# Closing a kernel without a block: engines run straight from the main program, closing waits in issue order, the last store waited for at the very end

## Chip, cores, metric

One core of one Trainium2 chip. The metric is the device time of one execution in microseconds (us). The profile's span, from the first instruction recorded to the last, is a little shorter than that time (the difference: "time minus span"). Every run quoted here is fast, with a mean granted TensorE clock of 0.997 or more.

## The reference, cut to what matters

Tokens x (2048 x 640) go through linear attention with 32 heads of 20 and through a gated feed-forward network of width 1728; a gate mixes the two.

```python
g = sigmoid((x * gate_w).sum(-1, keepdims=True))
a = A_ref(x, A_wqkv, A_w_phi, A_wo)     # q, k, v; softmax features; kv state; num / den; wo
b = (gelu(x @ w_gate) * (x @ w_up)) @ w_down
return g * a + (1 - g) * b
```

## The kernel before

The kernel records each operation through a small helper, which adds the waits: a semaphore counts each engine's finished operations, and each DMA takes one of 16 "lanes" of SyncE in turn, each lane with its own semaphore. `finish` makes one engine wait for everything. In the code, `_Ev` is a semaphore together with the value that it has to reach. All of it was written inside the SyncE part of a block (`nc.Block`).

```python
    def _wait(self, eng, ev):                      # skips what this engine has already waited for
        w = self.seen.setdefault(id(eng), {})
        if ev.value <= w.get(id(ev.sem), 0):
            return
        w[id(ev.sem)] = ev.value
        eng.wait_ge(ev.sem, ev.value)
    ...
    def finish(self, eng):                         # lanes 0..15 first, then the engines
        for q in self.queues.values():
            for L in q["lanes"]:
                if L["count"] > 0:
                    eng.wait_ge(L["sem"], L["count"])
        for e in self.engs.values():
            if e["count"] > 0:
                eng.wait_ge(e["sem"], e["count"])
    ...
    def run(self):
        nc = self.nc
        self.alloc()
        with nc.Block() as blk:
            @blk.sync
            def _(sp):
                self.sc = _Sched(nc, {"sp": (nc.sync, 16), "act": (nc.scalar, 4), "pool": (nc.gpsimd, 2)})
                self.loads()
                self.attention_state()
                self.ffn()
                self.sc.finish(sp)
```

The very last output tile is stored in two pieces; the second, 128 columns wide (32 KB), is the last store of the program, and it happens to use lane 7.

The softmax here doesn't subtract the row's maximum and nothing guards it: scores larger than these inputs give would overflow.

Of the kernel before, what the change touches and what calls it, by code (L numbers as in the profile page):

```python
# [11 lines left out]
class _Ev:  # L12
    __slots__ = ("sem", "value", "ekey")

    def __init__(self, sem, value, ekey=None):
        self.sem = sem
        self.value = value
        self.ekey = ekey


class _Sched:


    def __init__(self, nc, dma_lanes):
        self.nc = nc
        self.engs = {}
        for key, obj in (("pe", nc.tensor), ("act", nc.scalar), ("dve", nc.vector), ("pool", nc.gpsimd)):
            self.engs[key] = {"obj": obj, "sem": nc.alloc_semaphore(f"ev_{key}"), "count": 0}
        self.queues = {}
        for q, (eng, nl) in dma_lanes.items():  # L30
            lanes = [{"sem": nc.alloc_semaphore(f"dq_{q}_{i}"), "count": 0} for i in range(nl)]
            self.queues[q] = {"lanes": lanes, "rr": 0, "eng": eng}
        self.seen = {}
        self.bufs = {}

    def _wait(self, eng, ev):
        w = self.seen.setdefault(id(eng), {})
# [4 lines that stand above are left out]
# [39 lines left out]
    def dma(self, qkey, fn, reads=(), writes=(), guard=()):  # L81
        q = self.queues[qkey]
        lane = q["rr"]
        q["rr"] = (lane + 1) % len(q["lanes"])
        L = q["lanes"][lane]
        if L["count"] > 0:
            self._wait(q["eng"], _Ev(L["sem"], L["count"]))
        for ev in self._hazards(reads, list(writes) + list(guard)):
            self._wait(q["eng"], ev)
        fn(q["eng"]).then_inc(L["sem"], 16)  # L90
        L["count"] += 16
        self._record(reads, writes, (qkey, lane), _Ev(L["sem"], L["count"]))

    def finish(self, eng):
        for q in self.queues.values():
            for L in q["lanes"]:
                if L["count"] > 0:
                    eng.wait_ge(L["sem"], L["count"])
        for e in self.engs.values():
            if e["count"] > 0:  # L100
                eng.wait_ge(e["sem"], e["count"])


class _Kernel:
# [22 lines left out]
    def run(self):  # L127
        nc = self.nc
        self.alloc()
        with nc.Block() as blk:  # L130
            @blk.sync
            def _(sp):
                self.sc = _Sched(nc, {"sp": (nc.sync, 16), "act": (nc.scalar, 4), "pool": (nc.gpsimd, 2)})
                self.loads()
                self.attention_state()
                self.ffn()
                self.sc.finish(sp)

    def alloc(self):
        nc = self.nc  # L140
# [669 lines left out]
```

## Time and profile before

| | before |
|---|---|
| time, median of the 3 runs known at first | 299.86 us (299.65 to 300.2) |
| span of the profiled run | 297.8 us |
| TensorE busy | 98% of the span |
| TensorE's last matmul starts | 294.85 us |
| last store issued / its semaphore complete | 295.55 / 296.99 us |
| last instruction ends | 297.82 us |

From the page of the kernel before: span, TensorE's row, and the chain of waits that ended last.

```profile
span 297.8 us, 4821 instructions
PE 292.9 (98%) x1913; PEld 171.9 (58%) x1913; DVE 162.2 (54%) x318; ACT 104.3 (35%) x183; POOL 29.0 (10%) x58
PE 96%; DMA 1%; ACT 1%; issue 0%; SPq 0%; ACTq 0%
```

TensorE bounds everything between the first and the last matmul. So a change that touches no compute has to look for its gain at the two ends.

What SyncE waited for in the last 14 us, kernel before (waiting line, what released it, us in total, times, longest; two waits for the last results before the store are left out):

```profile
...
SPq L98 <- DMA out_dram<-outsb: 0.9, 1, 0.9
SPq L130 <- PEq L130: 0.2, 1, 0.2
```

L98 is the lane loop of `finish`, L101 its engine loop, L130 the block. Their instructions in the kernel before (engine, operation, count, nanoseconds min/median/max, first and last start in us), line by line:

```profile
L98 SPq EVENT_SEMAPHORE  x7: 17/28/842, 295.9 to 297.1; - x7
L101 SPq EVENT_SEMAPHORE  x4: 28/28/28, 297.2 to 297.3; - x4
L130 POOLq EVENT_SEMAPHORE  x2: 17/17/17, 297.6 to 297.7; - x2
...
L130 SPq COMPARE_BRANCH  x1: 41/41/41, 297.4 to 297.4; - x1
L130 SPq DRAIN  x1: 13/13/13, 297.6 to 297.6; - x1
L130 SPq EVENT_SEMAPHORE  x1: 17/17/17, 297.8 to 297.8; - x1
...
L130 PEldq EVENT_SEMAPHORE  x1: 51/51/51, 297.8 to 297.8; - x1
```

One of the seven L98 waits lasts 842 ns: that is the wait that really waits, for the last store. The other ten find their semaphores long reached, and yet they take time. The records of the trace, in order, make it plain (the compiler packs up to two waits into an instruction):

```
start us   ns   kernel before, SyncE unless noted
295.546   333   issue of the last store
295.924    17   wait            } four waits that pass at once
...                             }
296.170   842   wait, holds lane 7 (last store); lane 7 completes at 296.990
297.044    28   wait            } six waits that pass at once,
...                             } 61 ns from start to start
297.348    28   wait            }
297.413    41   branch out of the block (holds one more wait)
297.590    13   drain, start of the closing barrier of five engines
297.765    51   last release of the barrier, on TensorE; ends 297.816
```

From the landing of the last store to the end of the span: 0.83 us in which no data is computed or moved.

### The profile page before, as it was taken

To read this page: it belongs to the slowest core of one execution; us is meant where nothing else is said; L and a number is where in the kernel's file an instruction comes from. 1 tells how busy PE (TensorE), PEld (TensorE's weight loads), DVE (VectorE), ACT (ScalarE), POOL (GpSimd) and SP (SyncE) were. 2 spreads that over 40 slices of the span, in tenths; PEclk is the share of its full clock that TensorE was granted. 3 is DMA by queue.
4 is the path that set the end of the run, shared out by engine and by line. 5 is a ranking of instruction groups with operands and counts; after the bars stand their busy time and mean duration, and the time that the engine had idled before them with its cause. 6 is when DMAs were issued, how large, how long until landed. Compare 5 with 4: busy or idle time off the path is not lost.

```text
span 297.8 us, 4821 instructions
## 1 busy us (share of the span) xinstructions
PE 292.9 (98%) x1913; PEld 171.9 (58%) x1913; DVE 162.2 (54%) x318; ACT 104.3 (35%) x183; POOL 29.0 (10%) x58
## 2 busy tenths in 40 slices
PE   7999999999999999999999999999999999999996
PEld 3576656555544556775555577655457765545763
DVE  1348999998875679514655700455580045567000
ACT  3367787576663221121222212122221212232111
POOL 7000000000000011201011100101110010111000
PEclk9999999999999999999999999999999999999999
DMA  7999990000002122112011200201101010110101
GB/s 219 211 209 335 355 350 18 0 0 2 0 2 53 35 20 28 47 44 66 3 22 22 20 27 24 60 6 25 22 9 37 22 46 23 22 24 0 44 24 44
DMA packets 38098, 18.77 MB, mean 63 GB/s; under 512 B 30203, under 2 KB 37820, under 8 KB 38076
## 3 DMA queue, kind: packets, MB, share of 16 engines
q1 hardware_dynamic: 37424, 18.44, 24.4%
q8 instruction: 15, 0.25, 0.3%
q10 hardware_dynamic: 652, 0.03, 0.1%
q14 instruction: 7, 0.06, 0.1%
HBM read 8.96 MB, written 2.62 MB: 39 GB/s over the span
## 4 chain that ended last, share of the span: by engine, by line
PE 96%; DMA 1%; ACT 1%; issue 0%; SPq 0%; ACTq 0%
PE ps L616 37%; PE ps L694 20%; PE ps L359 13%; PE ps L700 7%; PE ps L504 7%; PE ps L649 4%; PE ps L452 3%; PE ps L368 2%; PE ps L626 1%; DMA xtok<-in_A_x_dram 1%; PE ps L339 1%; ACT Eq L510 1%; ACT Ek L418 0%; PE ps L284 0%; PE ps L304 0%
## 5 line engine op out<-in xcount | busy, mean ns | idle before, releaser
L616 PE MATMUL ps<-xT,wu_sb 128*128 128x512 bf16 x260 | 64.6, 379 | 0.2 <-ACT Eq L510 0.2
L616 PE MATMUL ps<-xT,wg_sb 128*128 128x512 bf16 x260 | 64.6, 379 | 0.0
L694 PE MATMUL ps<-wd_sb,hT 128*128 128x320 bf16 (+2 forms) x448 | 63.6, 299 | 0.0
L621 DVE TENSOR_TENSOR hT<-ps,gl 128x512 bf16<-128x512 f32 x52 | 35.7, 688 | 44.5 <-PE ps L616 44.4
L619 ACT ACTIVATE gl<-ps 128x512 bf16<-128x512 f32 x52 | 31.1, 597 | 80.8 <-PE ps L616 78.6
L694 PEld LDWEIGHTS ps<-wd_sb,hT 128*128 128x128 bf16 x448 | 43.2, 98 | 17.8
L616 PEld LDWEIGHTS ps<-xT,wu_sb 128*128 128x128 bf16 x260 | 25.4, 98 | 31.1 <-issue 0.7
L359 PE MATMUL ps<-w,xT 128*128 128x512 bf16 (+3 forms) x240 | 40.9, 321 | 0.0
L616 PEld LDWEIGHTS ps<-xT,wg_sb 128*128 128x128 bf16 x260 | 25.0, 98 | 27.2
L710 ACT ACTIVATE outsb<-ps,Gm 128x640 bf16<-128x640 f32 (+2 forms) x17 | 13.0, 763 | 74.7 <-PE ps L700 74.7
L678 POOL TENSOR_TENSOR Og<-O,O 128x640 bf16<-128x640 bf16 x16 | 22.3, 1394 | 167.5 <-DVE O L676 167.5
L359 PEld LDWEIGHTS ps<-w,xT 128*128 128x128 bf16 x240 | 22.4, 97 | 18.2
L665 DVE RECIPROCAL RH<-ps 128x32 f32<-128x32 f32 x16 | 5.7, 358 | 40.7 <-PE ps L649 39.7
L429 DVE TENSOR_REDUCE Dk<-Ek 128x64 f32<-128x1280 bf16 x16 | 23.7, 1480 | 3.2 <-ACT gcol L421 3.2
L438 DVE TENSOR_TENSOR Ek<-Ek,Dk 128x640 bf16<-128x640 bf16 x32 | 25.0, 821 | 0.6
L504 PE MATMUL ps<-xT,wq 128*128 128x512 bf16 x100 | 24.7, 379 | 0.3 <-ACT Eq L510 0.3
L676 DVE TENSOR_TENSOR O<-ps,RH 128x640 bf16<-128x640 f32 x32 | 24.8, 816 | 0.0
L700 PE MATMUL ps<-wo_sb,goT 128*128 128x320 bf16 (+2 forms) x160 | 24.5, 299 | 0.0
L510 ACT ACTIVATE Eq<-ps 128x512 bf16<-128x512 f32 x40 | 21.7, 604 | 4.0 <-PE ps L504 4.0
L418 ACT ACTIVATE Ek<-ps 128x640 bf16<-128x640 f32 x32 | 20.7, 702 | 3.5 <-PE ps L359 3.5
L700 PEld LDWEIGHTS ps<-wo_sb,goT 128*128 128x128 bf16 x160 | 15.5, 98 | 6.3
L649 PEld LDWEIGHTS ps<-KV,Eq 128*128 128x128 bf16 x192 | 12.0, 98 | 3.1
(66 smaller groups left out, 154.2 us busy)
## 6 DMA issues: line engine op xcount, KB each, us to landing
out_dram<-outsb SPq DMA_DIRECT2D x15, 160.0 KB, 2.0
wd_sb<-in_B_w_down_dram SPq DMA_DIRECT2D x1, 2080.0 KB, 12.4
wg_sb<-in_B_w_gate_dram SPq DMA_DIRECT2D x1, 1120.0 KB, 5.7
wu_sb<-in_B_w_up_dram SPq DMA_DIRECT2D x1, 1120.0 KB, 9.6
wg_sb<-in_B_w_gate_dram SPq DMA_DIRECT2D x1, 960.0 KB, 9.9
wu_sb<-in_B_w_up_dram SPq DMA_DIRECT2D x1, 960.0 KB, 10.2
w<-in_A_wqkv_dram SPq DMA_DIRECT2D x5, 160.0 KB, 4.0
wo_sb<-in_A_wo_dram SPq DMA_DIRECT2D x1, 800.0 KB, 10.1
```

Source lines behind the costliest of these rows:

```text
L359: sc.op("pe", lambda e, kt=kt: e.matmul(self.bank(bank)[:, bcol:bcol + n], self.xT[:, kt, t * P:(t + 1) * P], self.w3[:, kt, c0:c0 + n], s ...
L429: sc.op("dve", lambda e: e.tensor_reduce(self.Dk[:, se, 0, :].rearrange("p (s h) -> p s h", h=H), self.Ek[:, se, :, :].rearrange("p s (h d ...
L438: sc.op("dve", lambda e, v=v, r=r: e.tensor_tensor(v, v, r, ALU.mult), reads=[("Rk", se)], writes=[("Ek", se, s)])
L504: sc.op("pe", lambda e, kt=kt: e.matmul(self.bank(bank), self.wq2[:, kt, i * P:(i + 1) * P], self.xT[:, kt, b * self.BT:(b + 1) * self.BT] ...
L510: sc.op("act", lambda e, s=s, scale=scale: e.activation(self.Eq[:, s, i, b * self.BT:(b + 1) * self.BT], self.bank(bank), AF.Exp, scale=sc ...
L616: sc.op("pe", lambda e, kt=kt, w=w, bk=bk: e.matmul(self.bank(bk), w[:, kt, c * P:(c + 1) * P], xs(kt), start=(kt == 0), stop=(kt == self. ...
L619: sc.op("act", lambda e: e.activation(self.gl[:, slot, :], self.bank(banks[0]), AF.Gelu_apprx_tanh), reads=[("ps", banks[0])], writes=[("g ...
L621: sc.op("dve", lambda e: e.tensor_tensor(self.hT[:, c, :], self.bank(banks[1]), self.gl[:, slot, :], ALU.mult), reads=[("ps", banks[1]), ( ...
L649: sc.op("pe", lambda e, s=s, i=i, n=n, o0=o0, k0=k0, bk=bk, r=r: e.matmul(self.bank(bk)[:, o0:o0 + n], self.Eq[:, s, i, t * P:(t + 1) * P] ...
L676: dve(lambda e, o=o, f=f, s=s: e.tensor_tensor(o, V[s][:, :, :, 0:DH], f, ALU.mult), rb + [key(6 + s)], [("O", s, sl)], guard=old)
L694: sc.op("pe", lambda e: e.matmul(self.bank(bk, w), self.hT[:, c, tt * P:(tt + 1) * P], self.wd_sb[:, c, w0:w0 + w], start=(c == 0), stop=F ...
L700: sc.op("pe", lambda e: e.matmul(self.bank(bk, w), self.goT[:, gs, k, :], self.wo_sb[:, k, w0:w0 + w], start=False, stop=(k == self.KD - 1 ...
```

## The change

Its intent: drop the block with its branches and its closing barrier, and arrange the closing waits so that those for old things come first and run while the last store is still under way.

```diff
@@ dma()
         L["count"] += 16
+        self.issued += 1
+        L["last"] = self.issued
@@
     def finish(self, eng):
-        for q in self.queues.values():
-            for L in q["lanes"]:
-                if L["count"] > 0:
-                    eng.wait_ge(L["sem"], L["count"])
         for e in self.engs.values():
             if e["count"] > 0:
-                eng.wait_ge(e["sem"], e["count"])
+                self._wait(eng, _Ev(e["sem"], e["count"]))
+        lanes = [L for q in self.queues.values() for L in q["lanes"] if L["count"] > 0]
+        for L in sorted(lanes, key=lambda L: L["last"]):
+            self._wait(eng, _Ev(L["sem"], L["count"]))
@@ run()
-        with nc.Block() as blk:
-            @blk.sync
-            def _(sp):
-                self.sc = _Sched(...)
-                ... the same calls ...
-                self.sc.finish(sp)
+        self.sc = _Sched(...)
+        ... the same calls ...
+        self.sc.finish(nc.sync)
```

Instruction order and waits of TensorE, VectorE, ScalarE and GpSimd do not change, except that their closing drain and barrier go.

More of the change, by code (lines that the diff above doesn't have):

```diff
@@ L34, in __init__ @@
         self.bufs = {}
+        self.issued = 0
     def _wait(self, eng, ev):
@@ L129, in run @@
         self.alloc()
-        with nc.Block() as blk:
-            @blk.sync
-            def _(sp):
-                self.sc = _Sched(nc, {"sp": (nc.sync, 16), "act": (nc.scalar, 4), "pool": (nc.gpsimd, 2)})
-                self.loads()
-                self.attention_state()
-                self.ffn()
-                self.sc.finish(sp)
+        self.sc = _Sched(nc, {"sp": (nc.sync, 16), "act": (nc.scalar, 4), "pool": (nc.gpsimd, 2)})
+        self.loads()
+        self.attention_state()
+        self.ffn()
+        self.sc.finish(nc.sync)
     def alloc(self):
```

## The prediction

> **What bounds the kernel.** TensorE: the page gives PE 292.9 us busy of a span of 297.8 (98%), and the chain of waits is 96% PE, at a granted clock of nine tenths or more throughout. Outside it lie the head (first matmul at 1.26 us) and the tail. TensorE's last matmul ends near 295.08 us. The records of the last 3 us then show: last eviction on ACT 295.11 to 295.47; SyncE wakes at 295.50, issues the last store (32 KB) 295.55 to 295.88; its last packet ends at 296.65, its semaphore lands at 296.99. From there to 297.82 us (0.83 us) nothing is computed or moved.
>
> **What those 0.83 us are.** SyncE's closing waits are 11 event-semaphore instructions, mostly with two semaphores each, 61 ns from start to start when nothing holds them. In lane order, four pass at once (295.92 to 296.11), the fifth holds the last store's lane and stands from 296.17 for 842 ns until 297.01, and six follow, 297.04 to 297.38, for what was long done: about 0.38 us. Then the branch out of the block with one more wait (297.41; the next instruction starts 177 ns later), and the block's closing barrier of all five engines, 297.59 to 297.82: 0.23 us.
>
> **What the change does.** Order and waits of PE, DVE, ACT and POOL stay; only their closing drain and barrier go. SyncE loses the branch in, the branch out, drain and barrier, and has 10 closing waits instead of 11 and a branch: engine counters already seen are skipped, lanes come oldest store first, the last store is in the last wait. The nine before it cost an estimated 9 x 61 = 0.55 us from 295.93, so end near 296.48, before the last landing at 296.99: hidden. The program then ends with the wait on the last store, at about 297.01. Saving: 297.82 - 297.01 = 0.8 us.
>
> **The head gives nothing.** SyncE's first load starts at 0.804 us, ACT's at 0.802, POOL's first memset at 0.803, and only SyncE branches. The Trainium skill ("Runtime: NRT & Kernel Launch", Instruction fetch mechanics) says a taken branch to a target outside the fetched window forces a fetch; the head shows no such stall, the tail at most 0.12 us (177 ns against 61). The opening barrier (0 to 0.74 us) stays.
>
> **On the critical path:** all 0.8 us, since it follows the last landing. 0.8 of 299.86 is 0.27%: within 2%.
>
> **Predicted time:** 299.86 - 0.8 = 299.05 us; range 298.6 to 299.5 (the three runs before spread by 0.55 us). The measured time is 1.8 us over the span; the same page lists barriers and resets around a kernel, and if engines that finish early get ahead there, one or two tenths more may go. Faster by over 2%: 1%; within 2%: 98%; slower by over 2%: 1%.
>
> **What would show it right.** Span near 297.0; no drain or barrier after the last landing; SyncE's last instruction a wait standing about half a microsecond, ending 0.02 us after the landing; nine short waits before it; head and TensorE's busy time unchanged within 0.2 us.
>
> **What would make it wrong.** The final barrier's work reappearing outside the span, so that the span falls and the time does not; shifted instruction positions stalling TensorE by tenths; run noise as large as the effect; the last store's landing (1.4 us here) varying by more than the saving.

## The result, and the profile after

| | before | after |
|---|---|---|
| time, median of 5 runs | 299.86 us (299.58 to 300.2) | 298.95 us (298.48 to 299.33) |
| ratio, fast runs | | 0.9971, 95% interval 0.9957 to 0.9985 |
| span of the profiled run | 297.8 us | 297.7 us |
| time of the profiled run | 299.61 us | 299.33 us |
| last landing to end of span | 0.83 us | 0.045 us |

Ratios are the mean time of one kernel's fast runs over that of the other's in the same rounds, so not quite the ratio of the medians quoted.

The kernel is 0.3% faster, within the 2% that count as the same. But the two profiled spans differ by only 0.1 us. The lines of the page after, to set beside those of before:

```profile
span 297.7 us, 4808 instructions
PE 293.5 (99%) x1913; PEld 172.4 (58%) x1913; DVE 162.3 (55%) x318; ACT 104.2 (35%) x183; POOL 29.0 (10%) x58
PE 93%; SPq 2%; DMA 2%; ACT 1%; issue 0%; ACTq 0%
```

The closing part did what was asked. SyncE's waits in the last 14 us, and the whole of its closing waits (L42 is now the one line of every wait; the first of the eleven is the wait ahead of the last store):

```profile
...
SPq L42 <- DMA out_dram<-outsb: 0.5, 1, 0.5
```

```profile
L42 SPq EVENT_SEMAPHORE  x11: 17/28/28, 296.2 to 297.7; - x11
```

```
start us   ns   kernel after, SyncE
296.246   332   issue of the last store
296.625    17   wait            } eight waits, 61 ns from start to start
...                             }
297.050    28   wait            }
297.173    28   wait, holds lane 6 (last store but one, complete at 297.156)
297.700    28   wait, holds lane 7 (last store, complete at 297.683); end 297.728
```

From landing to end it is 45 ns. But everything from the last store back sits 0.70 us later than before. That shift arises in the first 16 us. The chain of waits up to 16 us, kernel before (start us, length us, what):

```profile
1.26 4.14 DMA xtok<-in_A_x_dram
5.41 0.04 issue
5.45 0.73 PE ps L284 x10
6.18 3.27 PE ps L368 x24
...
12.26 2.71 PE ps L359 x20
14.98 0.02 issue
14.99 0.80 PE ps L339 x12
```

and kernel after:

```profile
4.21 4.32 SPq L228
8.52 0.05 issue
8.57 7.08 DMA wkT<-in_A_wqkv_dram
15.65 0.05 issue
15.69 0.80 PE ps L338 x12
```

The first "fold" (L339 before, L338 after), which multiplies the transposed key weights `wkT`, starts at 14.99 us in one and 15.69 in the other. In the profile after, TensorE was already 0.26 us behind when it began its last matmul before the fold (15.02 against 14.76 us); it then stood idle for 0.46 us, until `wkT` had landed, against 0.02 in the profile before. Did the change do this, or did the profile catch a slow run? The profiled run of the changed kernel was the slowest of its five (299.33 us; spans of the five: 297.7, 297.2, 296.9, 297.4, 297.4). The experiments had to answer that, and one more thing: time minus span was 1.8 us before and 1.6 after, so 0.2 us were saved outside the span, where the page shows nothing.

### The profile page after: what moved, and what is told of

Same layout as the page of the kernel before. It is cut to its first block, busy times and chain, and to the rows that moved or that the text cites. A ratio compares the mean times of both kernels' runs of the same rounds, so it can differ in the third digit from the quotient of the medians.

```text
span 297.7 us, 4808 instructions
## 1 busy us (share of the span) xinstructions
PE 293.5 (99%) x1913; PEld 172.4 (58%) x1913; DVE 162.3 (55%) x318; ACT 104.2 (35%) x183; POOL 29.0 (10%) x58
## 4 chain that ended last, share of the span: by engine, by line
PE 93%; SPq 2%; DMA 2%; ACT 1%; issue 0%; ACTq 0%
PE ps L615 37%; PE ps L693 20%; PE ps L358 12%; PE ps L699 7%; PE ps L503 7%; PE ps L648 4%; PE ps L451 3%; DMA wkT<-in_A_wqkv_dram 2%; SPq L228 1%; PE ps L625 1%; PE ps L338 1%; SPq L215 1%; ACT Eq L509 1%; ACT Ek L417 0%; SPq L211 0%
```

## The experiments

Theory: two separate costs stood behind the last landing, the six late waits and the block's branch and barrier; 0.2 us more go outside the span because engines that finish early get ahead there; the shift in the head is run-to-run variation. Rivals: only one of the two costs counts; the 0.2 us belong to the barrier as such; removing the block disturbs the head.

All kernels that were run, each timed in five rounds (n includes the profiled run where it was one more). The experiments ran in four groups; each group shared one chip and the runs of before on it. "Minus before" is the mean time less that of the runs of before in the same rounds. "Landing to end" is read from each kernel's one profile.

| kernel | n | mean time | minus before | mean span | time minus span | landing to end |
|---|---|---|---|---|---|---|
| before, all runs that list a span | 48 | 299.90 | | 298.10 | 1.80 (1.74 to 1.86) | 0.82 |
| after, first result | 5 | 298.90 | -0.95 | 297.32 | 1.58 | 0.045 |
| after_again | 6 | 298.88 | -1.03 | 297.27 | 1.61 | 0.045 |
| block_neworder | 5 | 299.50 | -0.41 | 297.68 | 1.82 | 0.485 |
| noblock_oldorder | 5 | 299.02 | -0.89 | 297.42 | 1.60 | 0.447 |
| reversed | 5 | 299.01 | -0.75 | 297.40 | 1.61 | 0.143 |
| all_wait_last | 5 | 299.11 | -0.65 | 297.38 | 1.73 | 0.079 |
| pe_wait_last | 5 | 299.20 | -0.56 | 297.32 | 1.88 | 0.080 |
| not_pe_wait | 6 | 298.88 | -1.15 | 297.12 | 1.76 | 0.048 |
| barriers8 | 6 | 301.99 | +2.23 | 300.15 | 1.84 | 2.811 |
| wv_on_act | 6 | 299.32 | -0.71 | 297.73 | 1.58 | 0.045 |
| wv_on_act_fin | 6 | 299.43 | -0.61 | 297.82 | 1.61 | 0.045 |
| fin_only | 5 | 298.81 | -1.12 | 297.20 | 1.61 | 0.045 |

How to read it: the spans of one and the same kernel scatter with a standard deviation of 0.39 us (the 48 runs of before), so a mean over five has a standard error near 0.17. Time minus span scatters by a few hundredths, and landing to end came out alike where it was profiled twice (0.826 and 0.821 in before, 0.045 and 0.045 in after). In every run of an experiment the output was correct.

### before_again and after_again: the same two kernels once more

No edit.

> The kernel before, unchanged, as a control and for the span of each of its runs. Theory (tail): time equal to before within 0.1%; spans near 298.0 on average with a spread of some tenths, because the load phase varies from run to run; time minus span 1.8 us in each run; from the last store's landing to the end of the span 0.83 us. Rival (the change moved work out of the span or slowed the body): the spans of before cluster at 297.8 and are not above those of after by 0.7.

> The changed kernel once more. Theory (tail): span about 0.75 us below that of the control on average, landing to end about 0.05 us, time minus span 1.6 us as in its first five runs. In the profile the start of the first fold (15.0 us in before, 15.7 in after) falls somewhere between 14.9 and 15.8, not tied to the kernel. Rival (removing the block shifts the body): the first fold starts near 15.7 again and the first transpose issue on SyncE takes 4.3 us again, against 3.8 in the control.

Measured: before_again has the ratio 1.0001 (0.9985 to 1.0017) to before, and six spans from 297.7 to 299.0. after_again has 0.9968 (0.9954 to 0.9982) and spans from 296.9 to 297.9. Its first fold starts at 15.85 us with a first transpose issue of 4.52 us, so by this profile alone the rival, that the change shifts the head, would have stood. The spans refute it. In all 14 profiles the time from the first fold to the last matmul is 279.84 to 279.86 us, so all scatter of the span lies before the first fold (or behind the last landing). Taking the span, less landing to end, less 282.00 us (279.86 + 0.70 + 1.44, last matmul to issue to landing), gives each run's first fold: on average 15.28 us for the 48 runs of before and 15.25 for the 11 of after. The difference of 0.03 us lies within its standard error of about 0.1, so no shift of the head is seen; two profiled runs in a row happened to be late ones. The profiles of the other kernels say the same: without a block the first fold starts anywhere between 14.99 us (fin_only) and 15.85, with the block between 14.98 and 15.56.

### block_neworder: only the order of the waits

```diff
+        with nc.Block() as blk:            # the block of before, around the
+            @blk.sync                      # calls and the new finish
+            def _(sp):
```

> Only the new order of the closing waits, block kept. Theory: landing to end falls from 0.83 to about 0.44 us (last wait 0.05, branch 0.18, barrier 0.23); time about 0.4 us below the control, 299.45; time minus span stays 1.8, as the closing barrier is still there. Rival (the order of the waits is worth nothing and all of it is the block): time as the control, landing to end 0.8.

Measured: landing to end 0.485 us (expected 0.44), time minus span 1.82, time 0.41 us below before. The block's lines in its profile; the wait for the last store is now the last wait before the branch:

```profile
L132 SPq COMPARE_BRANCH  x1: 41/41/41, 297.6 to 297.6; - x1
L132 SPq DRAIN  x1: 13/13/13, 297.8 to 297.8; - x1
...
L132 PEldq EVENT_SEMAPHORE  x1: 51/51/51, 298.0 to 298.0; - x1
```

The order of the waits alone is worth 0.826 - 0.485 = 0.34 us.

### noblock_oldorder: only the block removed

```diff
-        with nc.Block() as blk:
-            @blk.sync
-            def _(sp):                     # the old finish stays
```

> Only the block removed, the old order of the closing waits kept. The last store's wait is now the fourth of eleven, seven follow. Theory: landing to end about 0.46 us (0.02 + 7 x 0.061), no barrier; time minus span 1.6 because the other engines run out earlier; time 0.4 us (span) plus 0.2 (outside) below the control, about 299.3. Rival (the waits are worth everything): time as the control.

Measured: landing to end 0.447 us (expected 0.46), time minus span 1.60. The wait for the last store lasts 890 ns in its profile, and seven more follow it:

```profile
L98 SPq EVENT_SEMAPHORE  x7: 28/28/890, 296.0 to 297.2; - x7
L101 SPq EVENT_SEMAPHORE  x4: 28/28/28, 297.3 to 297.4; - x4
```

The time, 299.02 us, is lower than the 299.3 expected: the mean span fell by 0.69 us, of which 0.38 is seen in the tail, and the rest is within the scatter of the head. The block alone is worth 0.826 - 0.447 = 0.38 us within the span, and the 0.2 us outside it go with the block, not with the order. The two parts sum to 0.72; together they gave 0.78. The missing 0.06 us is one wait: without the branch, the wait that rode on it needs an instruction of its own, so here seven waits come late instead of six. Both costs are real, so neither rival stands.

### reversed: the last store's wait first

```diff
-        for L in sorted(lanes, key=lambda L: L["last"]):
+        for L in sorted(lanes, key=lambda L: L["last"], reverse=True):
```

> The changed kernel with its closing waits in the opposite order, last store first (eighth of ten instructions is not reached before it; the last store's lane is held from the first two). Theory (every wait instruction behind the landing costs 61 ns): landing to end 0.02 + about 9 x 0.061 = 0.55 to 0.6 us instead of 0.045; time minus span 1.6; time about 0.5 us over the changed kernel, 299.4. If instead the order of waits costs nothing: landing to end under 0.1. (Waits are packed in pairs by the compiler, so the last store's wait may stand as late as the eighth instruction; then two follow and landing to end is about 0.15 us.)

Measured: landing to end 0.143 us. The case in parentheses came true: the compiler pairs waits, and the one written first came out in the eighth of ten instructions; two followed, 60 ns each. The main figure of 0.55 to 0.6 us was thus not tested by this edit. What follows: the cost per late wait holds (the wait for the last store ended 0.021 us after the landing, and 0.143 - 0.021 = 0.122 us for the two behind it is 61 ns each), and the place of a wait must be read from the built program, not from the source.

### barriers8: eight barriers more

```diff
         self.sc.finish(nc.sync)
+        for _ in range(8):
+            nc.all_engine_barrier()
```

> The changed kernel with eight barriers of all engines after its end. Theory: each costs about 0.2 us from one to the next (the single one of before took 0.23 from drain to end), together 1.6 to 1.9 us of span, and time minus span is 1.8 again, as after one barrier; time about 300.6 to 301.0. Rival (a barrier costs nothing on an idle core): time as the changed kernel.

Measured: landing to end 2.811 us, that is 2.77 us for eight, time 2.23 us over before, time minus span 1.84. SyncE's part of the eight:

```profile
L138 SPq DRAIN  x8: 7/7/13, 297.1 to 299.6; - x8
L138 SPq EVENT_SEMAPHORE  x8: 17/17/17, 297.3 to 299.8; - x8
```

The expectation was too low: back to back they come every 0.33 us (one took 0.53), not every 0.2, because a repeated barrier also contains the drains of all engines after the last release (in the records the five drains of the second barrier run from 297.34 to 297.47 us, between one release at 297.31 and the next at 297.63). A barrier on an idle core is not free, and the time shows it in full.

### all_wait_last, pe_wait_last, not_pe_wait: who must end early outside the span

```diff
+        L = max(lanes, key=lambda L: L["last"])
+        for e in self.engs.values():                # all_wait_last
+            self._wait(e["obj"], _Ev(L["sem"], L["count"]))
+        # pe_wait_last: the same for PE alone; not_pe_wait: for ACT, DVE and POOL
```

> The changed kernel, but PE, ACT, DVE and POOL also wait for the last store at their very end, with no barrier. Theory (early engines get ahead outside the span): time minus span goes back from 1.6 to 1.8 us although there is no barrier; landing to end stays under 0.1; time about 0.2 us over the changed kernel, 299.1. Rival (the 0.2 us outside the span belong to the block's barrier or branch as such): time minus span stays 1.6, time as the changed kernel.

> As the one before, but only PE waits for the last store. If TensorE's closing work is what takes the 0.2 us outside the span: time minus span 1.8. If it is another engine's, or the sum of several: 1.6, or between the two.

> The changed kernel, but ACT, DVE and POOL wait for the last store at their end and PE does not. Theory (the 0.2 us outside the span are TensorE's closing work, which starts early only without the block): time minus span 1.6 us, as in the changed kernel (with PE waiting it was 1.84 to 1.92). Rival (any engine that ends late costs it): 1.7 to 1.9.

Measured, time minus span: all wait 1.73 (1.67 to 1.79), PE alone 1.88 (1.84 to 1.92), all but PE 1.76 (1.73 to 1.80); where only SyncE ends late it was 1.55 to 1.64 in after and after_again. So the 0.2 us are not the barrier's or the branch's own: without either, keeping other engines in the program until the last landing brings most of them back or more (the 16 runs lie between 1.67 and 1.92). That they belong to TensorE alone is refuted by not_pe_wait.

Where they lie can be read from the traces, although `prof` does not print it: the packed traces keep the semaphores' updates after the last instruction. Semaphore 2, which no instruction of the kernel touches, is updated in two passes of nine, and between the start of the one and the start of the other more than 200 other semaphores are updated (us from the end of the span):

| | before | after | all_wait_last | pe_wait_last | not_pe_wait |
|---|---|---|---|---|---|
| updates of the first pass that came before the end | 0 | 4 | 0 | 0 | 1 |
| first pass ends | 0.77 | 0.29 | 0.78 | 0.55 | 0.81 |
| longest step within the second pass | 0.13 | 0.46 | 0.10 | 0.48 | 0.10 |
| second pass ends | 2.00 | 1.80 | 1.95 | 2.07 | 1.96 |

The last row, less time minus span, is 0.18 to 0.21 us in 13 of the 14 profiles (0.07 in barriers8, which stays unexplained), so the 0.2 us are in these passes. In after, engines that had finished early made four of the nine first updates 1.36 to 1.78 us before the end, while SyncE still waited for the last store, and the first pass ended 0.48 us sooner. The second pass then contains one long step and gives 0.28 us of this back. PE alone is the dearest case because its first pass is late and the long step remains. What the long step is the traces do not show. The Trainium skill ("Runtime: NRT & Kernel Launch", The ~15µs preamble/postamble breakdown) lists barriers and semaphore resets that the runtime puts after a kernel; that the passes and the updates between them are these is inferred, since the traces hold no instruction for them.

### wv_on_act and wv_on_act_fin: can the head be steadied?

```diff
-            sc.dma("sp", lambda e: e.dma_start(self.w3[:, kt, 0:D], ...
+            sc.dma("sp" if kt < 2 else "act", lambda e: e.dma_start(self.w3[:, kt, 0:D], ...
+            "act": (nc.scalar, 6)                  # 6 lanes for ACT instead of 4
 # wv_on_act_fin also: the last store on a semaphore of its own
+            "fin": (nc.sync, 1)
-            sc.dma("sp", lambda e: e.dma_start(rows[:, w0:w0 + n], ...
+            sc.dma("fin" if last and w0 else "sp", lambda e: e.dma_start(rows[:, w0:w0 + n], ...
```

> The changed kernel with three of the five loads of the value weights issued by ACT instead of SyncE, so that SyncE's transposing loads start about 1.4 us earlier. Theory (all of the run-to-run variation of the span is the landing of the transposed key weights, which decides when the first fold starts: 14.98 to 15.85 us in the profiles so far, and from there to the last matmul it was 279.86 us in every one): the first fold starts with TensorE as its limit, at 14.9 to 15.0, in every run; spans 296.9 to 297.1 in all runs, spread under 0.2 instead of 1; mean time about 0.3 us under the changed kernel, 298.6. Rival (the variation lies elsewhere): spread as before. If the loads of the value weights arrive later from ACT, the first stage gets slower and the fold starts after 15.2.

> As the one before, and the last store has a semaphore of its own, so that it waits for one semaphore instead of two and needs no wait instruction ahead. Theory: from the start of the last matmul to the issue of the last store 0.65 instead of 0.70 us, the rest alike; time 0.05 us below the one before, which five rounds cannot tell from none. The best version if the one before holds: about 298.55.

Measured: slower than the changed kernel, mean spans 297.73 and 297.82 against 297.3, though narrower (297.5 to 297.9 in wv_on_act). The expected gain failed by the reason that was set down as its risk. TensorE in wv_on_act (start us, us, what, idle before it):

```profile
6.48 0.97 PE L367 MATMUL ps<-w,xT 128*128 128x480 bf16 x6 [0.17 <-DMA w<-in_A_wqkv_dram]
7.75 2.63 PE L367 MATMUL ps<-w,xT 128*128 128x480 bf16 x18 [0.30 <-DMA w<-in_A_wqkv_dram]
```

With the transposing loads started earlier (2.76 us instead of 4.2), the value weights came late, and the first fold was held back by TensorE's own work at 15.75 us instead of by `wkT`. Earlier transposing loads were paid for with later value weights; the order of before is the better one.

The profiles also refute "all of it is `wkT`". In block_neworder the fold starts late too, at 15.56, and there TensorE was late by itself. Its twenty 128-column transposes, which follow the warm-up matmuls, are slower:

```profile
4.44 2.31 PE L286 MATMUL ps<-ident,xtok 128*128 128x128 bf16 x20
6.55 3.49 PE L370 MATMUL ps<-w,xT 128*128 128x480 bf16 x24
```

and in the kernel before:

```profile
4.40 0.73 PE L284 MATMUL ps<-ident,xtok 128*128 128x128 bf16 x10
5.45 0.73 PE L284 MATMUL ps<-ident,xtok 128*128 128x128 bf16 x10 [0.32 <-DMA xtok<-in_A_x_dram]
6.02 3.44 PE L368 MATMUL ps<-w,xT 128*128 128x480 bf16 x24
```

Their weight loads start 107 ns apart in the one and 56 ns apart in the other, and in other profiles the step from 107 to 56 falls in between. In block_neworder `wkT` was late as well (it landed at 15.52, and the fold followed 46 ns later), but TensorE alone would not have begun the fold before 15.40, estimated as the start of its last matmul before it, 15.34, plus the usual step of 55 ns; the same estimate gives 14.82 in before. The clean case is all_wait_last: `wkT` landed at 13.40 us, the fold began at 15.57, 55 ns after the matmul ahead of it, and its chain of waits from the first matmul up to the fold holds TensorE alone (start us, length us, what; L286 has the transposes, and the rest up to the fold is TensorE too):

```profile
1.26 3.17 PE ps L535 x7
4.42 0.01 issue
4.43 2.31 PE ps L286 x20
6.75 3.46 PE ps L370 x24
```

The Trainium skill ("TensorE: Matmul & The Clock Gate", Part 1: The HAM clock gate) states 106.7 and 55.6 ns from start to start of matmuls of 128 columns at half and full clock, and that the window that decides on the step is free-running, so that its moment varies from run to run. The traces agree with both figures (the matmuls' starts show them too), and with a moment that is not tied to the kernel: in their record of the granted clock, the full clock begins at 4.19 us in before, 4.76 in before_again and 6.65 in block_neworder. So the scatter has two sources, the clock step and the landings of the loads. In nine of the 14 profiles the fold began 46 or 47 ns after `wkT` landed, in the other five 55 ns after the matmul ahead of it. How much each source has in all runs was not separated.

### fin_only: the version to keep

Only the second edit above, on the changed kernel.

> The changed kernel with all loads as they were, and only a semaphore of its own for the last store, so that it needs no wait instruction ahead. Expected from the run with both changes: last matmul to issue 0.65 instead of 0.70 us, issue to landing 1.44, landing to end 0.045, time minus span 1.6; time 0.05 us below the changed kernel, 298.85, and within its noise. The version to keep if it is not slower.

Measured: from the last matmul to the issue of the last store 0.650 us (0.696 in after), landing to end 0.045; mean 298.81 us, ratio to before 0.9966 (0.9952 to 0.9980). The 0.05 us are seen in the profile and are too few for the timing to separate from the changed kernel. It beats before clearly, is not slower than the changed kernel, and is the one to keep.

## Why the prediction was right or wrong

- "Within 2%" and the range (298.6 to 299.5) held: 298.95 us against 299.05 predicted.
- "The program then ends with the wait on the last store": shown. Landing to end fell from 0.826 to 0.045 us, a saving of 0.78 against 0.8 predicted. Mean spans agree: 298.10 over 48 runs of before, 297.29 over 11 of after, 0.81 less. The wait ended 0.045 us after the landing, not 0.02.
- The split was right: 0.38 us of late waits and 0.18 + 0.23 of branch and barrier, against 0.34 and 0.38 when each is undone alone.
- "The nine before it ... hidden" held: the last of the nine passed at 297.17, the landing came at 297.68.
- The term mis-sized: the saving of 0.8 took no share outside the span and left "one or two tenths more" as a possibility. Measured, time minus span fell from 1.80 to 1.60, because engines that finish early do get ahead after their last instruction (the passes of semaphore 2 above), and the means differ by 1.0 us (299.90 to 298.89). Worked out with both terms, 299.90 - 0.78 - 0.20 = 298.92, so the point forecast was 0.13 us too high.
- "Span near 297.0", and "head ... unchanged within 0.2 us", failed for the profiled run: span 297.7, head 0.70 us later. The step that failed was to expect one profile to show 0.8 us; single runs scatter by 1.4 us in span (297.6 to 299.0 in before), in the head. Over many runs the head is unchanged within the noise: 15.28 and 15.25 us, worked out from the same spans, so this and the agreement of the mean spans are one piece of evidence and not two.
- "A wait standing about half a microsecond": the standing is there, as a gap of 0.5 us ahead of the last wait, not as its duration. See the last section.
- The head gives nothing from the branch in: SyncE's first load starts at 0.804 us in both.

## What to carry to other kernels

Look at what stands between the last store's landing and the last instruction: a satisfied wait cost 61 ns here, a block's branch and barrier 0.38 us. The first vanishes if old things are waited for while the last store is in flight, the second if the program ends without the block. For effects of a few tenths, compare stretches within the traces (first fold to last matmul, landing to end), since one profiled span against another can hide the whole effect. Let engines that have finished run out of the program; holding them until the end cost 0.13 to 0.28 us here, which no line of the profile shows.

## What the Trainium skill lacked or had wrong

- "Perfetto Trace Analysis" (Sequencer-only Instruction): it says the time spent waiting for a semaphore is not within the reported window. Here that depended on the pair: a wait instruction whose second semaphore was the late one was reported with 842 ns (before), 890 (noblock_oldorder) and 188 and 496 (reversed), so with the waiting; one whose first was late (after, block_neworder) showed 28 ns behind a gap of 0.5 us.
- "Runtime: NRT & Kernel Launch" (The ~15µs preamble/postamble breakdown): it gives the stages around a kernel, but not that their visible cost depends on who ends last. Time minus span was 1.60 us with SyncE alone, 1.76 with ACT, DVE and POOL besides, 1.88 with PE alone besides, 1.73 with all.
- The same page gives about 355 ns for the runtime's own pass over five engines; in the traces the nine updates of semaphore 2 just before each program take 0.37 us. The cost of a barrier inside the program is not there: 0.23 us from the last engine's drain to the end, 0.33 us each when repeated.
- No page was found to have the cost of a wait instruction whose semaphores have already reached their values: 58 to 59 ns on SyncE with one semaphore, about 61 with two.
- "TensorE: Matmul & The Clock Gate" (Part 1) advises to leave the ramp aside as under 1% of a span. That holds in size, but the whole effect studied here was 0.3%, and the ramp, with the landings, decided which of two profiles looked faster. The mean granted clock of the runs (1.0 in before and in after) does not show it.
